# Turning gathered tokens by VectorE's 32x32 blocks in the early slots and the first main slot of a routed attention and mixture-of-experts kernel

## The chip, the cores and the metric

One core of a Trainium2 chip runs the whole kernel. The metric is the device time of one execution in microseconds (us). The engines are named as in the profile: PE is TensorE (PEld its weight loads), ACT is ScalarE, DVE is VectorE, POOL is GpSimd, and SP only issues DMAs.

## The reference

Attention with a feature map is followed by a layer of eight experts, one expert to a token. Cut to what matters:

```python
def phi(x):                        # x: 8 x 8 heads x 576 tokens x 64
    proj = x @ w_phi               # 128 features
    proj -= max(abs(proj))
    return concat(exp(proj), exp(-proj))
kv, z = phi(k).T @ v, sum(phi(k))
x = phi(q) @ kv / (phi(q) @ z + 1e-6)          # then 4608 tokens x 512

logits = x @ w_gate                            # 8 experts
# a token takes its own best expert, or, where its local gate
# is 0.5 or more, the expert of the token before it
h = relu(x @ w1[e])                            # 512 -> 1024
out = softmax(logits)[e] * (h @ w2[e])         # 1024 -> 512
```

The tokens of each expert are listed on the chip, so which tokens an expert works on is known only when the kernel runs.

## The kernel before, in words

The first part, up to about 276 us, is the attention. Its results go to a table `xs` in device memory, one row of 512 numbers to a token. After every quarter of the tokens a gate (`gate`, line 699) finds each token's expert and rank and writes its number into the lists (`lst`, line 836, from GpSimd's queue).

The second part works on slots. A slot is one expert and up to four units of 128 tokens. Two early slots of three units each use the tokens of the first half, whose gates are done, so that TensorE has work while the last gate and the plan of the main slots (`plan_main`, line 996) are computed. Then come the main slots, of four, three, two units or one.

For each unit, `gather_x` (line 1217) fetches 128 rows of `xs` by an indirect DMA of GpSimd's queue into a tile `xg`, one token to a partition. The products need the transposed form, a feature to a partition, and in two parts, a rounded high part and the rest (`xhi`, `xlo`), since each product is made of three: high by high, high by low, low by high (`three`, line 1303). There are two ways to turn a unit:

- `whole` (line 1246): TensorE turns four pieces of 128x128 into a PSUM tile `tr` (line 1252), and `parts` (line 1293) has ScalarE cast it to `xhi` (line 1299) and VectorE subtract that to give `xlo` (line 1301).
- `turned_rows` (line 1265): VectorE turns every 32x32 block of the unit in one instruction, `blocks`, into a tile `z` (line 1273). Sixteen copies of 32 partitions by 128 elements, `places`, put the blocks where they belong (line 1285), four to each of the four `j`: even `j` on GpSimd, odd `j` on ScalarE. They are done in two halves of eight. `split` then calls `parts` on the result. TensorE has no part in it.

Before the change the first early slot's three units go through `first_tokens` (line 1238) and `whole`; the second early slot's three, and the first main slot's four, go through `whole`; all later units go through `turned_rows`. That is ten units by TensorE.

A slot's weights come in eight pieces of 128x1024, four for each layer, from SP's queue (line 1157). ScalarE casts a piece to its high half `whi` (line 1170), VectorE subtracts to get `wlo` (line 1173), in `split` (line 1161). `need` (line 1207) does this for all pieces that a layer still lacks, `spare` and `landed` (lines 1186 and 1202) for those that come while a layer runs.

The order of the work around the change is written by hand. `layer1` (line 1328) goes through eight blocks f of 128 hidden features; ScalarE makes the ReLU and the high part `hh` (line 1358), VectorE the low part `hl` (line 1359). In the middle of each block, and behind its ReLU, `pause` takes the next step off a list, sixteen in all: step 2f in the middle of block f, step 2f+1 behind it. `layer2` (line 1386) takes steps at f = 0 and f = 2 of each unit, six for three units, and what is left over runs behind it. `slots` (line 1428) hands these lists over: for the early slots, `soon` for layer 1 and `later` for layer 2, built at lines 185 to 208. In `soon` of the first early slot, `go` and `rest` advance the last gate; in `soon` of the second, `read` takes the main slots' lists from TensorE and the steps `a[0]` to `a[3]` gather the first main slot's units.

Each engine works through its own queue in order. The queues are filled by a scheduler that goes by the order in which the program issues its instructions and by when it expects them to be ready. `past(engine)` (line 1181) overrides it: what stands inside is put behind the last instruction noted for that engine in `marks`. ReLUs, block copies and casts of tokens set ScalarE's mark; line 1170 issues behind it:

```python
with self.past(self.act):          # line 1169
    self.act.copy(hi, raw)
```

Of the kernel before, what the change touches and what calls it, by code (L numbers as in the profile page):

```python
# [7 lines left out]
F32 = mybir.dt.float32  # L8
# [9 lines left out]
B, H, S, D = 8, 8, 576, 64  # L18
# [63 lines left out]
class Kernel:  # L82
# [9 lines left out]
    def run(self):  # L92
        nc, tc, A = self.nc, self.tc, self.A
        act, dve = self.act, self.dve
        with ExitStack() as root:
# [94 lines left out]

            def ahead(k):
                s = self.by_size[4][0]
                self.gather_x(s, k, self.marks[self.act] if k else None)
                if k == 0:
                    self.coming.append(s)
                if k == 3:
                    m.extend(self.tokens([s], True))
            a = [lambda k=k: ahead(k) for k in range(4)]

            def more():  # L200
                next(plan, None)

            def singles():
                more()
                m[0]()
            self.slots(self.eslots, soon=[[no, no, no, go, no, no, go, no, no, go, rest],
                                          [no] * 9 + [read, a[0], a[1], no, a[2], no, a[3]]],
                       later=[[listed], [no, no, singles] + [lambda k=k: m[k]() for k in (1, 2, 3)] + [more]])
            back.close()
            self.mid.close()  # L210
            self.open_rest(root)
# [1043 lines left out]
    def tokens(self, slots, late=False, after=None):  # L1255

        for s in slots:
            if "xg" not in s:
                self.gather_x(s, after=after)
        units = [(s, k) for s in slots for k in range(s["n"])]  # L1260
        if late:
            return [lambda s=s, k=k: self.whole(s, k, k % 3 == 2, self.here()) for s, k in units]
        return [self.turned_rows(s, k) for s, k in units]

    def turned_rows(self, s, k):

        e, x = {}, s["xg"][k]
        act, dve, pool, at = self.act, self.dve, self.pool, slice(k * 128, k * 128 + 128)

        def blocks():  # L1270
            e["z"] = self.ml1.tile([128, DM], F32, name="z", bufs=2)
            with self.past(dve):
                self.marks[dve] = dve.transpose(e["z"].rearrange("p (c t) -> p c t", t=32),  # L1273
                                                x.rearrange("p (c r) -> p c r", r=32))

        def places(half):
            z = e["z"].rearrange("p (a b t) -> p a b t", a=4, b=4)
            to = self.into(s)[0].bitcast(F32)[:, :, at] if len(s["ei"]) == 2 else x.rearrange("p (a t) -> p a t", a=4)
            for j in (2 * half, 2 * half + 1):
                for b in range(4):  # L1280
                    q, g = slice(32 * b, 32 * b + 32), slice(32 * j, 32 * j + 32)
                    engine = act if j % 2 else pool
                    with self.past(engine):
                        copy = act.copy if j % 2 else pool.tensor_copy
                        self.marks[engine] = copy(to[q, :, g], z[g, :, b, :])  # L1285

        def split():
            if len(s["ei"]) == 1:
                hi, lo = [y[:, :, at] for y in self.into(s)]
                self.parts(s, hi, lo, slice(0, 128), x.rearrange("p (a t) -> p a t", a=4))  # L1290
        return blocks, lambda: places(0), lambda: places(1), split
# [136 lines left out]
    def slots(self, order, held=None, soon=(), later=()):  # L1428
# [19 lines left out]
        for i, s in enumerate(order):  # L1448
# [2 lines left out]
            self.need(s, 4)  # L1451
            new = order[i + 1] if i + 1 < len(order) else None
            rows = self.tokens(ahead[i], bool(soon) and i == 0, self.last_y if held is not None and i == 0 else None)
            first, rest = list(soon[i]) if i < len(soon) else [], rows
            if not soon and s["n"] > 1:
                some = [f for u in rows for f in u[0:3]]
                first = [lambda: None] * 16
# [146 lines left out]
```

## Time and profile before

| | us |
|---|---|
| median of 3 runs | 715.73 |
| lowest, highest run | 714.66, 718.45 |
| the profiled execution's own time | 712.14 |
| its span, first to last instruction | 710.3 |
| PE busy | 698.4 |
| DVE busy | 460.7 |
| ACT busy | 411.8 |
| POOL busy | 265.0 |

The profile is of one execution. Its span lies inside its own time; the rest is what surrounds the instructions. A row of the timeline gives the start, the duration, the engine, the line of the kernel, the operation with what it writes and reads, how often it follows itself, and in brackets how long the engine stood idle before and what ended that. TensorE's instructions overlap, so the time that one costs is read from start to start.

### The profile page before, as it was taken

The page shows a single profiled execution, that of the slowest core. Times are in us where ns is not written, and L with a number is a line of the kernel's source. Part 1 is how long each engine was busy: PE and PEld are TensorE (multiplying, and loading weights), DVE is VectorE, ACT ScalarE, POOL GpSimd, SP SyncE. Part 2 cuts the span into 40 slices and gives each one's busy share as a digit, 9 for nine tenths or more (in the row PEclk, how much of TensorE's full clock was granted, in tenths as well). Part 3 has the DMA queues.
Part 4 walks back from the last instruction along what each step waited for, and adds up shares of the span by engine and source line. Part 5 has one row for each costly group of instructions (what it writes and reads, how often), then busy time and mean ns, then how long its engine had stood idle before and what let it go on. Part 6 is the DMA issues. An engine that isn't in the chain of part 4 may idle for free. (4 is left out here: it accounts for less than half of the span.)

```text
span 710.3 us, 22974 instructions
## 1 busy us (share of the span) xinstructions
PE 698.4 (98%) x9576; PEld 617.9 (87%) x9576; DVE 460.7 (65%) x876; ACT 411.8 (58%) x888; POOL 265.0 (37%) x532
## 2 busy tenths in 40 slices
PE   7999999999999999999999999999999999999996
PEld 6999999999999999888887986889888877888985
DVE  6898899889998995683537446535643367554522
ACT  5777776777768873434465654745754269471512
POOL 0211101430146675562345551345744236443311
PEclk9999999999999999999999999999999999999998
DMA  7855545555466863254818975344886375444200
GB/s 232 268 154 148 160 124 155 148 149 161 134 183 198 252 189 113 64 181 129 280 70 294 405 279 194 135 149 150 265 307 252 110 243 172 150 163 155 76 27 31
DMA packets 66074, 125.17 MB, mean 176 GB/s; under 512 B 7180, under 2 KB 45260, under 8 KB 65910
## 3 DMA queue, kind: packets, MB, share of 16 engines
q1 hardware_dynamic: 57680, 100.90, 44.8%
q0 software_dynamic: 7968, 22.58, 9.0%
q8 instruction: 76, 1.25, 0.7%
q14 instruction: 30, 0.25, 0.1%
q10 hardware_dynamic: 320, 0.20, 0.1%
HBM read 102.11 MB, written 21.80 MB: 174 GB/s over the span
## 5 line engine op out<-in xcount | busy, mean ns | idle before, releaser
L1173 DVE TENSOR_TENSOR wlo<-wraw,whi 128x1024 fp32r<-128x1024 f32 x80 | 96.4, 1222 | 37.8 <-ACT whi L1170 37.5
L1305 PE MATMUL l<-whi,hh 128*128 128x512 f32 (+1 forms) x288 | 113.4, 394 | 0.5 <-ACT hh L1358 0.5
L1306 PE MATMUL l<-wlo,hh 128*128 128x512 f32 (+1 forms) x288 | 112.7, 391 | 0.8 <-DVE wlo L1173 0.8
L1307 PE MATMUL l<-whi,hl 128*128 128x512 f32 (+1 forms) x288 | 112.6, 391 | 0.0
L362 ACT ACTIVATE kp<-sb 128x512 f32<-128x512 f32 x144 | 83.3, 623 | 48.9 <-DVE sb L359 48.1
L1359 DVE SCALAR_TENSOR_TENSOR hl<-l,hh 128x512 fp32r<-128x512 f32 (+3 forms) x84 | 50.4, 600 | 93.2 <-ACT hh L1358 93.1
L1170 ACT CAST whi<-wraw 128x1024 fp32r<-128x1024 f32 x80 | 82.4, 1047 | 43.8 <-PE l L1307 27.0
L1358 ACT ACTIVATE hh<-l 128x512 fp32r<-128x512 f32 (+3 forms) x84 | 44.0, 525 | 108.9 <-PE l L1307 57.2
L1305 PE MATMUL l<-xhi,whi 128*128 128x384 f32 (+4 forms) x308 | 106.8, 347 | 0.0
L1307 PE MATMUL l<-xhi,wlo 128*128 128x384 f32 (+4 forms) x308 | 106.5, 346 | 0.0
L1306 PE MATMUL l<-xlo,whi 128*128 128x384 f32 (+4 forms) x308 | 106.4, 345 | 0.0
L358 DVE TENSOR_REDUCE m<-pj 128x8 f32<-128x1024 f32 (+1 forms) x74 | 88.3, 1193 | 20.4 <-PE pj L351 18.3
L1285 POOL COPY xg<-z 32x128 f32<-32x128 f32 x208 | 70.4, 339 | 58.7 <-DVE z L1273 41.4
L359 DVE TENSOR_TENSOR sb<-pj,m 128x1024 f32<-128x1024 f32 (+1 forms) x74 | 88.5, 1196 | 5.6
L351 PE MATMUL pj<-first,kq 64*128 64x128 f32 x1152 | 85.3, 289 | 3.5 <-DMA first<-in_first 3.4
L483 PE MATMUL nm<-kvs,qp 128*64 128x73 f32 x2304 | 86.3, 227 | 0.5 <-issue 0.4
L1419 POOL DMA_INDIRECT out<-y,p_tokm x31 | 37.4, 1205 | 127.2 <-DVE y L1413 126.0
L386 ACT ACTIVATE qp<-pj 128x512 f32<-128x512 f32 x144 | 78.1, 596 | 8.4 <-PE pj L371 7.5
L483 PEld LDWEIGHTS nm<-kvs,qp 128*64 128x64 f32 x2304 | 79.1, 137 | 1.0 <-issue 0.7
L351 PEld LDWEIGHTS pj<-first,kq 64*128 64x128 f32 x1152 | 71.4, 190 | 9.4 <-DMA first<-in_first 3.4
L403 PE MATMUL kvp<-v,kp 128*64 128x65 f32 x2048 | 75.3, 224 | 0.1
L1285 ACT COPY xg<-z 32x128 f32<-32x128 f32 x208 | 61.7, 296 | 20.3 <-DVE z L1273 16.0
(266 smaller groups left out, 1080.0 us busy)
## 6 DMA issues: line engine op xcount, KB each, us to landing
wraw<-in_w1h SPq DMA_DIRECT2D x44, 512.0 KB, 5.1
wraw<-in_w2h SPq DMA_DIRECT2D x44, 512.0 KB, 5.6
kq<-in_kqT SPq DMA_DIRECT2D x47, 384.0 KB, 4.1
v<-in_va SPq DMA_DIRECT2D x48, 195.0 KB, 3.5
xs<-xo SPq DMA_DIRECT2D x48, 128.0 KB, 2.4
whi<-in_w1h SPq DMA_DIRECT2D x8, 512.0 KB, 5.8
wlo<-in_w1h SPq DMA_DIRECT2D x8, 512.0 KB, 8.6
whi<-in_w2h SPq DMA_DIRECT2D x8, 512.0 KB, 7.2
```

The source lines that it names most:

```text
L351: self.last_pe = self.pe.matmul((q if j else t)[:, h, i % 2, j, :], kq[r, j, s], self.w2[r], start=True, stop=True)
L358: dve.tensor_reduce(m[:, a:a + n], x[:, s], AX.X, ALU.max, apply_absolute_value=True)
L359: self.last_dve = dve.tensor_sub(to[:, s], x[:, s], m[:, a:a + n].unsqueeze(2).broadcast_to([128, n, 128]))
L362: self.last_act = act.activation(kp[:, :, :, sg, :].rearrange("p c h f -> p h c f"), sb[:, :, :, 0], AF.Exp, scale=1.0 - 2 * sg)
L386: self.act.activation(qp[:, sg].rearrange("p h (c r k) -> p (h c) r k", c=2, r=2), src, AF.Exp, scale=1.0 - 2 * sg)
L483: self.last_num = self.pe.matmul(e["t"][r, c - c0, k], self.ch[i]["qp"][:, sg, h, q0 + r.start:q0 + r.stop], kvs[:, sg, k], start=sg == 0, ...
L1170: self.act.copy(hi, raw)
L1173: (low or self.dve).tensor_sub(lo[:, c], raw[:, c], hi.bitcast(F32)[:, c])
L1285: self.marks[engine] = copy(to[q, :, g], z[g, :, b, :])
L1305: mm(o, ah, bh, start=first, stop=False)
L1306: mm(o, ah, bl, start=False, stop=False)
L1307: self.last_pe = mm(o, al, bh, start=False, stop=last)
```

## The change

The second early slot's three units, and units 0 to 2 of the first main slot, go through `turned_rows`; unit 3 of the first main slot stays with TensorE. `turned_rows` gets a string `who` with one letter for each of the sixteen copies, in order: a for ScalarE, p for GpSimd, v for VectorE. The early units get twelve a and four v, six a and two v to each half. The main units get five p and three a in the first half, four and four in the second. The string for all later units gives the engines that they had.

The tile `z` of these units lies in the attention's memory, in place of its `kvs` tiles (`blank`). The steps are spread over the lists: the early units' blocks and halves at steps 2, 3, 5, 6, 7, 9, 10, 11 and 13 of the first early slot's layer 1, behind what stood there, and their splits in its layer 2, where `whole` stood. The gathers of the first main slot move to steps 10 to 13 of the second early slot's layer 1 and no longer wait for ScalarE's mark; unit 0's blocks and first half are step 14, its second half step 15, the last of that layer. The rest goes to the second early slot's layer 2: in the table, m is a unit's number in the first main slot.

| step of layer 2 | before | after |
|---|---|---|
| unit 0, f = 0 | nothing | m1 blocks, first half |
| unit 0, f = 2 | nothing | m1 second half |
| unit 1, f = 0 | plan goes on, m0 by TensorE | plan goes on, m2 blocks |
| unit 1, f = 2 | m1 by TensorE | m2 first half, m0 split |
| unit 2, f = 0 | m2 by TensorE | m2 second half, m1 split |
| unit 2, f = 2 | m3 by TensorE | m3 by TensorE |
| behind the layer | plan goes on | m2 split, plan goes on |

```diff
--- before.py
+++ after.py
@@ -190,22 +190,26 @@
 
             def ahead(k):
                 s = self.by_size[4][0]
-                self.gather_x(s, k, self.marks[self.act] if k else None)
+                self.gather_x(s, k)
                 if k == 0:
                     self.coming.append(s)
-                if k == 3:
-                    m.extend(self.tokens([s], True))
+                m.append(self.turned_rows(s, k, "pappappapapapapa") if k < 3 else
+                         lambda: self.whole(s, k, True, self.here()))
             a = [lambda k=k: ahead(k) for k in range(4)]
+
+            def do(*steps):
+                return lambda: [m[k][i]() for k, i in steps]
 
             def more():
                 next(plan, None)
 
             def singles():
                 more()
-                m[0]()
-            self.slots(self.eslots, soon=[[no, no, no, go, no, no, go, no, no, go, rest],
-                                          [no] * 9 + [read, a[0], a[1], no, a[2], no, a[3]]],
-                       later=[[listed], [no, no, singles] + [lambda k=k: m[k]() for k in (1, 2, 3)] + [more]])
+                m[2][0]()
+            self.slots(self.eslots, soon=[[no, no, no, go, no, no, go, no, no, go, rest] + [no] * 5,
+                                          [no] * 9 + [read, a[0], a[1], a[2], a[3], do((0, 0), (0, 1)), do((0, 2))]],
+                       later=[[listed], [do((1, 0), (1, 1)), do((1, 2)), singles, do((2, 1), (0, 3)),
+                                         do((2, 2), (1, 3)), lambda: m[3](), do((2, 3)), more]])
             back.close()
             self.mid.close()
             self.open_rest(root)
@@ -1258,17 +1262,21 @@
             if "xg" not in s:
                 self.gather_x(s, after=after)
         units = [(s, k) for s in slots for k in range(s["n"])]
-        if late:
-            return [lambda s=s, k=k: self.whole(s, k, k % 3 == 2, self.here()) for s, k in units]
-        return [self.turned_rows(s, k) for s, k in units]
-
-    def turned_rows(self, s, k):
+        return [self.turned_rows(s, k, "avaaavaaaaavaaav") if late else self.turned_rows(s, k) for s, k in units]
+
+    def blank(self):
+        if hasattr(self, "ml1"):
+            return self.ml1.tile([128, DM], F32, name="z", bufs=2)
+        z = self.back2.tile([128, 2, 2 * (KW + D + 1)], F32, name="z", tag="kvs", bufs=3)
+        return z.rearrange("p s k -> p (s k)")[:, 0:DM]
+
+    def turned_rows(self, s, k, who="ppppaaaappppaaaa"):
 
         e, x = {}, s["xg"][k]
         act, dve, pool, at = self.act, self.dve, self.pool, slice(k * 128, k * 128 + 128)
 
         def blocks():
-            e["z"] = self.ml1.tile([128, DM], F32, name="z", bufs=2)
+            e["z"] = self.blank()
             with self.past(dve):
                 self.marks[dve] = dve.transpose(e["z"].rearrange("p (c t) -> p c t", t=32),
                                                 x.rearrange("p (c r) -> p c r", r=32))
@@ -1279,9 +1287,9 @@
             for j in (2 * half, 2 * half + 1):
                 for b in range(4):
                     q, g = slice(32 * b, 32 * b + 32), slice(32 * j, 32 * j + 32)
-                    engine = act if j % 2 else pool
+                    engine, copy = {"a": (act, act.copy), "p": (pool, pool.tensor_copy),
+                                    "v": (dve, dve.tensor_copy)}[who[4 * j + b]]
                     with self.past(engine):
-                        copy = act.copy if j % 2 else pool.tensor_copy
                         self.marks[engine] = copy(to[q, :, g], z[g, :, b, :])
 
         def split():
@@ -1451,7 +1459,10 @@
             self.need(s, 4)
             new = order[i + 1] if i + 1 < len(order) else None
             rows = self.tokens(ahead[i], bool(soon) and i == 0, self.last_y if held is not None and i == 0 else None)
-            first, rest = list(soon[i]) if i < len(soon) else [], rows
+            first, rest = list(soon[i]) if i < len(soon) else [], [u[3] for u in rows]
+            if soon and rows:
+                for k, f in zip((2, 3, 5, 6, 7, 9, 10, 11, 13), [f for u in rows for f in u[0:3]]):
+                    first[k] = lambda f=f, g=first[k]: (g(), f())
             if not soon and s["n"] > 1:
                 some = [f for u in rows for f in u[0:3]]
                 first = [lambda: None] * 16
```

## Rows read from the trace of the kernel before

**Rows 1.** The page, part 1: busy us (share of the span) xinstructions
```profile
PE 698.4 (98%) x9576; PEld 617.9 (87%) x9576; DVE 460.7 (65%) x876; ACT 411.8 (58%) x888; POOL 265.0 (37%) x532
```

**Rows 2.** TensorE's waits, whole span: line, releaser, us in total, times, longest
```profile
PE l L1306 <- DVE wlo L1173: 0.8, 1, 0.8
```

**Rows 3.** Two stretches: length; busy of PE, PEld, DVE, ACT, POOL; clock, DMA, GB/s
```profile
276.00:294.00 18.00, 18.00 (x111) 17.19 (x112) 10.51 (x43) 3.60 (x8) 9.19 (x13) 1.00 0.08 23
329.20:348.00 18.80, 18.80 (x91) 15.11 (x90) 12.40 (x13) 11.69 (x16) 5.12 (x4) 1.00 0.76 232
```

**Rows 4.** Timeline: start, us, engine, line, operation, [idle before]; TensorE around one group
```profile
300.60 0.39 PE L1307 MATMUL l<-whi,hl 128*128 128x512 f32 x1
...
300.83 0.60 PE L1252 MATMUL tr<-first,xg 128*128 128x128 f32 x4
...
301.50 0.40 PE L1306 MATMUL l<-wlo,hh 128*128 128x512 f32 x1
```

**Rows 5.** Timeline, first main layer 1: ScalarE's, GpSimd's copies, VectorE's block turn
```profile
359.01 1.23 ACT L1285 COPY xg<-z 32x128 f32<-32x128 f32 x4 [7.32 <-DVE z L1273]
...
359.10 2.58 POOL L1285 COPY xg<-z 32x128 f32<-32x128 f32 x8 [5.44 <-PE l L1306]
...
358.26 0.71 DVE L1273 STREAM_TRANSPOSE z<-xg 128x512 f32<-128x512 f32 x1 [5.85 <-DMA xg<-xs,p_tokm]
```

**Rows 6.** Timeline, first early slot's layer 1: two of ScalarE's ReLUs
```profile
282.54 0.49 ACT L1358 ACTIVATE hh<-l 128x384 fp32r<-128x384 f32 x1 [1.71 <-PE l L1307]
...
287.05 0.49 ACT L1358 ACTIVATE hh<-l 128x384 fp32r<-128x384 f32 x1 [1.60 <-PE l L1307]
```

**Rows 7.** Timeline, same stretch: casts in the gate's chain on VectorE
```profile
284.64 0.22 DVE L78 CAST g_ef<-g_ci 9x128 f32<-9x128 int32 x1
...
288.05 0.19 DVE L78 CAST g_ohb<-g_oh 128x72 bf16<-128x72 f32 x1
```

**Rows 8.** Timeline, same stretch: TensorE takes the one-hot matrix
```profile
288.62 0.21 PE L780 MATMUL pt<-g_ohb,consts 128*128 128x72 bf16 x1
```

**Rows 9.** Timeline, GpSimd: the main slots' list, and unit 0's gather
```profile
316.32 0.92 POOL L902 DMA_INDIRECT lr<-lst,p_rim  x1 [0.31 <-issue]
...
323.44 0.98 POOL L1223 DMA_INDIRECT xg<-xs,p_tokm  x1 [6.20 <-DVE p_probm L673]
```

**Rows 10.** Timeline, TensorE: it takes that list
```profile
322.52 0.41 PE L933 MATMUL pt<-first,lr 34*128 34x34 f32 x2
```

**Rows 11.** Tile xg, 320 to 332 us: landing of the main slot's four gathers
```profile
DMA to landing us min/median/max: 3.3/3.3/4.2
```

**Rows 12.** Timeline, end of the second early slot's layer 1: ScalarE
```profile
329.40 0.49 ACT L1358 ACTIVATE hh<-l 128x384 fp32r<-128x384 f32 x1 [1.59 <-PE l L1307]
329.79 2.93 ACT L1170 CAST whi<-wraw 128x1024 fp32r<-128x1024 f32 x3
```

**Rows 13.** Timeline, same stretch: VectorE
```profile
327.85 0.56 DVE L1359 SCALAR_TENSOR_TENSOR hl<-l,hh 128x384 fp32r<-128x384 f32 x1 [1.52 <-ACT hh L1358]
...
330.86 3.50 DVE L1173 TENSOR_TENSOR wlo<-wraw,whi 128x1024 fp32r<-128x1024 f32 x3 [0.38 <-ACT whi L1170]
```

**Rows 14.** Timeline, same stretch: TensorE's product with the low half, its weight load
```profile
332.14 0.19 PEld L1306 LDWEIGHTS l<-wlo,hh 128*128 128x128 f32 x1 [0.21 <-DVE wlo L1173]
332.19 0.45 PE L1306 MATMUL l<-wlo,hh 128*128 128x512 f32 x1
```

**Rows 15.** Timeline at 369 us: a subtraction and a GpSimd copy
```profile
369.08 1.18 DVE L1173 TENSOR_TENSOR wlo<-wraw,whi 128x1024 fp32r<-128x1024 f32 x1
...
369.22 1.20 POOL L1285 COPY xg<-z 32x128 f32<-32x128 f32 x1 [2.51 <-DVE z L1273]
```

**Rows 16.** Timeline, end of the second early slot: last token casts; main slot's first product
```profile
344.04 1.06 ACT L1299 CAST xhi<-tr 128x512 fp32r<-128x512 f32 x2
...
348.04 1.20 PE L1349 MATMUL l<-xhi,whi 128*128 128x512 f32 x4
```

**Rows 17.** Tile xg, 349 to 358 us: landing of the next slot's gathers
```profile
DMA to landing us min/median/max: 6.5/7.2/7.8
```

## The prediction

> **What bounds the kernel now.** I read the page's busy line first: TensorE is busy 98% of a 710.3 us span and the next engine, VectorE, 65% [rows 1]. A busy TensorE could still be waiting inside its instructions, so the second view is the list of its waits. The longest after the start is 0.8 us, once, for a low half of the weights [rows 2]. So the kernel ends when TensorE has issued its queue, and a change is worth what it takes out of that queue, less the waits that it puts in. The third view is the table by stretch: in the two where the change puts its copies, the granted clock is 1.00 (the 2.4 GHz level), so no clock can be won, and ScalarE and GpSimd have room: 3.6 and 9.2 of 18.0 us busy in the first early slot's layer 1, 11.7 and 5.1 of 18.8 us in the second early slot's layer 2 [rows 3]. The question is not whether the copies fit on average but which TensorE instruction comes behind one of them.
>
> **What is removed.** A unit of 128 tokens costs TensorE four transposes. Ten units are turned this way; the change takes six: three of the second early slot, three of the first main slot. From the product ahead of a group at 300.60 to the second product behind it at 301.50 are 0.90 us, for the group and two product starts; a start is 0.23 (300.60 to 300.83) [rows 4], so the group costs 0.90 - 0.46 = 0.44. The duration printed for the group, 0.60, overlaps its neighbours and is not used. Six groups: 6 x 0.44 = **2.64 us out of TensorE's queue**. The PSUM casts and subtractions behind the groups become casts and subtractions from SBUF, as many as before, in the same place in the queues: nothing.
>
> **What is added.** Six VectorE block turns of 0.71 us and 16 block copies a unit. Four copies took ScalarE 1.23, so 0.31 each; eight took GpSimd 2.58, so 0.32 each [rows 5]. The early units get 12 ScalarE and 4 VectorE copies each, the main units 9 GpSimd and 7 ScalarE. None is on TensorE; what they cost is what they delay.
>
> **First place: the last gate's chain.** Each hidden block f of the first early slot now has a half unit behind it: six ScalarE copies, 6 x 0.31 = 1.87, and a ReLU of 0.49: 2.36 us. Two blocks took 4.51 (282.54 to 287.05), 2.26 each [rows 6]; the copies begin behind the second block, and with the unequal blocks in between the ReLU of the fifth, at 287.05, comes some 0.4 late. VectorE's subtraction for that block stands ahead of the cast of the one-hot matrix on its in-order queue. The cast ended at 288.05 + 0.19 = 288.24 [rows 7], and TensorE took it at 288.62 [rows 8]: 0.38 of cover. VectorE also gets two copies of 32x128 near there. The trace has no such copy on VectorE; below, one costs 0.15 or so like its smallest operations, above, ScalarE's 0.31; I take 0.22, from the cast of 9x128 [rows 7]. So 0.4 + 0.44 - 0.38 = **0.45 us of new TensorE wait** (0 if the copies run behind the chain, 1.3 if the lags all add). The main slots' list, which this chain feeds, was fetched from 316.32 and taken by TensorE at 322.52 [rows 9, 10]; with a landing of 4.2, the longest of the token gathers just after [rows 11], it was there at 320.5. The 2.0 of cover pay for three groups fewer ahead of it (1.32, less the new 0.45) and for a chain that is later by as much: nothing.
>
> **Second place: the split of the weights.** Line 1170 casts the high half, line 1173 subtracts the low half. For the seventh piece of the second early slot the cast began at 329.79, right behind the ReLU of the last hidden block (329.40), as first of three [rows 12]; the low half was ready after 330.86 + 3.50/3 = 332.03 [rows 13]; the product with it came at 332.19, and its weight load had waited 0.2 [rows 14]. **There is no cover at all on this chain.** The new last step of that layer 1 puts four ScalarE copies of the main slot's unit 0 behind the same ReLU and makes the last of them the mark behind which line 1170 issues. So the cast, which is ready, waits for four copies: 4 x 0.31 = 1.24. Three more stand a step earlier, behind a block turn that itself goes behind the subtraction that ended at 327.85 + 0.56 = 328.41: turned at 329.11, copied by 330.05, which holds the ReLU from 329.40 to 330.05, 0.65. Together **1.9 us of new wait**. Bounds: 1.24 if the ReLU goes ahead, 2.6 if unit 1's block turn (0.71) also slips in ahead of the subtraction. What queues behind is TensorE's whole layer 2; the next piece follows 1.17 later and is needed 1.38 later (six starts), so it adds nothing.
>
> On GpSimd and VectorE together: the last turned unit of the next stage had one GpSimd copy of 1.20 instead of 0.32, beside a weight subtraction begun at 369.08 that kept its 1.18 [rows 15]. The Trainium skill, "SBUF — State Buffer", section "Who interferes with whom", says that a VectorE instruction with two SBUF inputs and a GpSimd instruction that reads SBUF take turns, and the second to issue blocks until the first ends. By that the row agrees on GpSimd's side; on VectorE's side the subtraction could wait for one copy too, 0.3 more in the sum. I leave that to the range, since no row shows the subtraction as the loser.
>
> **Third place: the start of the main slot.** The last cast of its tokens ended at 344.04 + 1.06 = 345.1, TensorE's first product was at 348.04 [rows 16]: 2.9 us of cover. ScalarE gains 18 copies, 5.6 us on 11.7, in 18.8: it fits with 1.5 to spare. I cost this at nothing; the cover is thin, and a rival below takes it away. The gathers of these units no longer wait for ScalarE and follow each other on GpSimd, so units 1 to 3 are issued sooner: nothing.
>
> **The sum.** -2.64 + 0.45 + 1.90 = -0.29. The profiled execution took 712.14 us (span 710.3 and 1.8 around it): 711.8 by the sum. It was below the median of the runs, 715.73, by 3.59; I carry that over: **715.4**. Half a per cent, 3.6 us, is about what a measurement of this kernel can tell from no change, and even the whole 2.64 is less.
>
> **The rivals.**
> - **The full gain** (chance 0.22): neither wait comes, because the block copies of unit 0 run before the ReLU, or the queues take the cast first. For it: ScalarE was idle 1.59 us ahead of that ReLU [rows 12], time enough for five copies. Against it: the mark puts the four copies ahead. 712.14 - 2.64 = 709.5 for the profile, 713.1 as median.
> - **GpSimd is late for the main slot** (0.15), the one that ends slower. Place: the last product operand of unit 2, ahead of 348.04. GpSimd was busy 5.1 us in the 18.8; 27 copies add 8.7; if each of a slot's eight weight subtractions costs it 0.9 as in [rows 15], 7.2 more: 21.0. From 18.8 on it decides: 2.2 us of wait at the main slot's first product on top of the sum, +1.9, 717.6. Against it: some copies start before 329.2, and not every subtraction need meet one. The page of the skill named above would make this the likely outcome if all eight meet copies.
> - **Unit 0's gather lands late** (0.08). It is issued at 323.44, and those four landed in 3.3 to 4.2 us [rows 9, 11]: by 327.6, ahead of the 328.41 from which the block turn could run. From 5.0 us on the landing decides. The gathers at 350 took up to 7.8 [rows 17]; then the turn starts at 331.2, and seven copies (2.2), the ReLU, the cast and the subtraction put the low half at 336.9: a wait of 4.7 instead of 1.9, 718.2. Against: the DMA engines are little used at 323.
> - **Another order on the queues** (0.05): the change moves marks, so later instructions may be placed otherwise. Not priced; either sign.
>
> The forecast keeps 0.50.
>
> **How the numbers follow.** The forecast with its bounds (0 to 1.3, 1.24 to 2.6) spans 714.3 to 717.2. To hold 8 in 10 the range goes down to the full gain with a little scatter, 712.8, and up to the late gather, 718.2. Faster by over 0.5% would need more than the groups hold, so only scatter on the full gain: 0.06. Slower by over 0.5% needs two of the waits together or an unforeseen order: 0.09. The rest, 0.85, is within.
>
> **What would show it.** Right: 16 TensorE transposes instead of 40; a TensorE wait of 1.2 to 2.6 us for a weight's low half (or high half) in the second early slot's layer 2, with ScalarE copies between the last ReLU and the cast; under 1.3 us of waits in the gate's chain; the stretch from the second group taken to the main slot's start otherwise shorter by 0.44 a group. Wrong: no such wait (then the full gain stands), a wait of TensorE for tokens at the main slot's first product (GpSimd), or a gain over 2.64 us, which nothing here explains.

## The result, and the profile after

The change made the kernel slower: 723.37 us as median of 7 runs (721.33 to 725.44) beside 717.61 of 7 runs of the kernel before (714.45 to 718.86), a ratio of 1.0098 with a 95% interval of 1.0073 to 1.0122. Here and below the ratio comes with its interval from the single runs; it is not the quotient of the two medians. The profiled execution took 723.37 us, its span 721.6. Forecast was no change that a measurement can tell.

The page of the kernel after, part 1 (busy us, share of the span, xinstructions), answers to [rows 1]:

```profile
PE 700.7 (97%) x9552; PEld 619.3 (86%) x9552; DVE 467.6 (65%) x894; ACT 428.8 (59%) x945; POOL 280.1 (39%) x559
```

TensorE issues 24 instructions fewer, so all six groups are gone, and still its busy time is up by 2.3: part of it ran at a lower clock, below. Lines have moved by 4 up to about line 1262 and by 8 behind it. TensorE's waits in the kernel after (line, releaser, us in total, times, longest), beside [rows 2]:

```profile
PE pt L937 <- DMA lr<-lst,p_r: 6.5, 1, 6.5
PE pj L355 <- DMA first<-in_first: 3.4, 1, 3.4
PE l L1313 <- ACT y L1423: 2.0, 1, 2.0
PE pt L937 <- DMA lr<-lst,p_rim: 0.8, 1, 0.8
PE l L1313 <- ACT whi L1174: 0.7, 1, 0.7
PE l L1315 <- issue: 0.7, 1, 0.7
PE pt L771 <- DVE g_ef L78: 0.4, 1, 0.4
```

The second one is the start of the kernel and was there before. The one that was forecast is the fifth, 0.7 for a weight's high half. The longest, 6.5, is for a list that the prediction never mentions: `p_r`, the rows of the last slots, fetched by `more` inside `singles` in the second early slot's layer 2 and handed to TensorE by the last step of that layer (`more` again). GpSimd's timeline, first of the kernel before, at the end of the second early slot:

```profile
336.01 1.02 POOL L1419 DMA_INDIRECT out<-y,p_toke  x1 [4.90 <-ACT y L1415]
337.33 1.88 POOL L902 DMA_INDIRECT lr<-lst,p_r  x1 [0.30 <-issue]
```

The same in the kernel after:

```profile
334.41 0.94 POOL L1293 COPY xg<-z 32x128 f32<-32x128 f32 x3 [0.90 <-DVE z L1281]
336.40 14.72 POOL L1293 COPY xg<-z 32x128 f32<-32x128 f32 x24 [1.05 <-DMA xg<-xs,p_tokm]
351.40 1.03 POOL L1427 DMA_INDIRECT out<-y,p_toke  x1 [0.28 <-POOL xg L1293]
352.73 1.03 POOL L906 DMA_INDIRECT lr<-lst,p_r  x1 [0.30 <-issue]
```

Before, the fetch stood 10.4 us ahead of TensorE's use of the list at 347.72. After, 24 block copies stand ahead of it on GpSimd's in-order queue, it is issued at 352.73, and TensorE, which had finished its layer, waits for it. Of the 15.4 us by which the fetch is later, 4.4 are the later start of the whole slot (first product at 316.43 for 312.00); 11.0 are its own. The copies are slow as well: 14.72 for 24, where 24 x 0.32 [rows 5] would be 7.7. The tile `xg` from 336 to 352 us (ns, min/median/max) shows how:

```profile
L1293 POOL COPY xg<-z x24: 285/289/1357, 336.4 to 349.8; 32x128 f32<-32x128 f32 x24
L1293 ACT COPY xg<-z x18: 294/296/300, 335.8 to 351.2; 32x128 f32<-32x128 f32 x18
```

Sixteen GpSimd copies keep 0.29; eight take 0.66 to 1.36. Those are the ones that meet one of VectorE's subtractions, six of the weights and two of the tokens, one copy to each. GpSimd's and VectorE's timeline, same stretch:

```profile
338.05 2.75 POOL L1293 COPY xg<-z 32x128 f32<-32x128 f32 x3
...
338.15 2.49 DVE L1177 TENSOR_TENSOR wlo<-wraw,whi 128x1024 fp32r<-128x1024 f32 x2 [0.54 <-ACT whi L1174]
```

Two subtractions of 1.25 each, and three copies in the same 2.75. The subtraction all but keeps its time (1.18 in [rows 15]). The Trainium skill, "SBUF — State Buffer", "Who interferes with whom", has a GpSimd instruction that reads SBUF and a VectorE instruction with two SBUF inputs exclude each other, and ScalarE never wait on anyone; both agree with these rows, ScalarE's 18 copies staying within 294 to 300 ns.

Behind the wait the products run slowly. TensorE, kernel after, with the next list and the three first blocks of the main slot:

```profile
359.26 0.38 PE L937 MATMUL pt<-first,lr 22*128 22x22 f32 x2 [6.51 <-DMA lr<-lst,p_r]
359.57 2.08 PE L1357 MATMUL l<-xhi,whi 128*128 128x512 f32 x4
361.44 1.91 PE L1357 MATMUL l<-xhi,wlo 128*128 128x512 f32 x4
363.15 1.46 PE L1357 MATMUL l<-xlo,whi 128*128 128x512 f32 x4
364.45 0.39 PE L1313 MATMUL l<-xhi,whi 128*128 128x512 f32 x1
```

And the table by stretch there (length; busy of PE, PEld, DVE, ACT, POOL with instructions; clock, DMA share, GB/s):

```profile
358.50:364.50 6.00, 5.24 (x15) 4.19 (x16) 0.27 (x2) 0.00 (x0) 3.14 (x4) 0.55 0.81 294
```

The granted clock is 0.55 on the mean, mostly the lower level of 1.2 GHz. Twelve products took 364.45 - 359.57 = 4.88, where they took 350.89 - 348.04 = 2.85 before: 2.0 us more.

By stages, from first product to first product: the first early slot took 36.13 before and 40.07 after (+3.9), the second 36.04 and 43.14 (+7.1), the main slot's twelve products 2.0 more. The second slot's +7.1 is 6.5 + 0.8 + 0.7 of waits less three groups; 0.5 is not accounted for. The three stages together are 13.0, more than the 11.3 between the spans; the remainder of the span was about 2 us shorter, and why is open. The first slot's +3.9 has waits of 0.4, 0.7 and 2.0 in it, the last of them here:

```profile
309.24 0.74 PE L1313 MATMUL l<-whi,hh 128*128 128x512 f32 x1 [1.98 <-ACT y L1423]
```

Behind it the granted clock was 0.50 from 309.3 to 312.7 us, which is some 1.7 more. How much of this is the change's is told by the runs.

### The profile page after: what moved, and what is told of

It is laid out like the page before. It is cut to its first block, busy times and chain, and to the rows that moved or that the text cites. A ratio compares the mean times of both kernels' runs of the same rounds, so it can differ in the third digit from the quotient of the medians.

```text
span 721.6 us, 23029 instructions
## 1 busy us (share of the span) xinstructions
PE 700.7 (97%) x9552; PEld 619.3 (86%) x9552; DVE 467.6 (65%) x894; ACT 428.8 (59%) x945; POOL 280.1 (39%) x559
## 3 DMA queue, kind: packets, MB, share of 16 engines
q8 instruction: 76, 1.25, 0.7%
## 5 line engine op out<-in xcount | busy, mean ns | idle before, releaser
L366 ACT ACTIVATE kp<-sb 128x512 f32<-128x512 f32 x144 | 83.3, 623 | 50.8 <-DVE sb L363 43.1
L1293 POOL COPY xg<-z 32x128 f32<-32x128 f32 x235 | 86.8, 369 | 62.0 <-DVE z L1281 43.8
L1293 ACT COPY xg<-z 32x128 f32<-32x128 f32 x265 | 78.5, 296 | 15.5 <-DVE z L1281 10.1
L390 ACT ACTIVATE qp<-pj 128x512 f32<-128x512 f32 x144 | 78.1, 595 | 8.6 <-PE pj L375 7.9
```

The costliest lines, as they stand in the source:

```text
L366: self.last_act = act.activation(kp[:, :, :, sg, :].rearrange("p c h f -> p h c f"), sb[:, :, :, 0], AF.Exp, scale=1.0 - 2 * sg)
L390: self.act.activation(qp[:, sg].rearrange("p h (c r k) -> p (h c) r k", c=2, r=2), src, AF.Exp, scale=1.0 - 2 * sg)
```

## The experiments

Four sets of kernels were run, each set together on one chip with the kernel before. The kernel before had a median of 715.45 (13 runs), 713.34 (24), 712.52 (28) and 716.98 (23) there.

**First set: the whole change again, and its two halves.** The first has no edit.

> The changed kernel once more, unaltered. In its first profile two things are to be told apart: TensorE's wait of 6.5 us for the last list (lr), and a stretch from 302.7 to 308.5 us in which VectorE's short operations of the plan come 0.5 us apart with one gap of 2.3, ScalarE's first output takes place at 308.50, and TensorE waits 0.7 and 2.0 us. Theory A: both belong to the order of the queues and come again, each within 0.5 us. Theory B: the stretch at 302.7 is a chance of that execution; then here VectorE's plan runs without gaps over 0.5 us there, TensorE has no wait of over 0.5 us between 296 and 312, and the time is some 3 to 4 us less.

724.65 us; the wait for the list 5.9, half the clock again behind it, for the other list 1.1, and the stretch is there again. Theory A, with the list's wait 0.6 apart where 0.5 was allowed.

For the next, the main slot goes back to TensorE:

```diff
-                m.append(self.turned_rows(s, k, "pappappapapapapa") if k < 3 else
-                         lambda: self.whole(s, k, True, self.here()))
+                m.append(lambda: self.whole(s, k, k % 3 == 2, self.here()))
-                m[2][0]()
+                m[0]()
```

with the gathers and steps of before.

> Only the second early slot's units go by blocks; the first main slot's by TensorE, as before. Theory (GpSimd's queue): the loss comes from the main units' copies on GpSimd, so the wait for the last list is gone here; three groups out of TensorE's queue are 1.3 us, the gate's chain puts 0.4 back: 0.5 to 1 us under the kernel before if the waits at 302 to 309 don't come. Rival (the early copies): these cost as much as in the changed kernel's first profile, 0.4 + 0.7 + 2.0 of waits and 1.7 of lower clock, less 1.3: 3 to 4 us over the kernel before.

718.45, ratio 1.0038 (1.0015 to 1.0062); no wait for `p_r`, but 1.1 for the list `p_rim` and waits of 0.3 to 1.0 in several other places. It is 3.0 over the kernel before, the rival's time. For the third, the early units go back to TensorE:

```diff
-        return [self.turned_rows(s, k, "avaaavaaaaavaaav") if late else self.turned_rows(s, k) for s, k in units]
+        if late:
+            return [lambda s=s, k=k: self.whole(s, k, k % 3 == 2, self.here()) for s, k in units]
+        return [self.turned_rows(s, k) for s, k in units]
```

and the lines that spread their steps over layer 1 are taken out.

> Only units 0 to 2 of the first main slot go by blocks; the second early slot's units by TensorE, as before. Theory (GpSimd's queue): the fetch of the last list stands behind 24 copies in a row again, TensorE waits 5 to 7 us for it, loses some 2 us more at the lower clock, and has 1.3 less to do: 5 to 8 us over the kernel before. Rival (the early copies make everything late): TensorE's wait for that list is under 1 us and the time within 2 us of the kernel before.

721.79, ratio 1.0084 (1.0060 to 1.0108), with a wait of 5.0 for `p_r` and half the clock behind it, 6.3 over the kernel before, as the theory had it. The main units by themselves make most of the loss. In the fourth the list's step goes ahead of the copies:

```diff
+            def fourth():
+                a[3]()
+                more()
             def singles():
-                more()
-                                          [no] * 9 + [read, a[0], a[1], a[2], a[3], do((0, 0), (0, 1)), do((0, 2))]],
+                                          [no] * 9 + [read, a[0], a[1], a[2], fourth, do((0, 0), (0, 1)), do((0, 2))]],
```

> The changed kernel, with the fetch of the last list issued with the gather of unit 3, ahead of all main copies on GpSimd, instead of behind them. Nothing else is taken away. Theory (GpSimd's queue): TensorE's 6.5 us wait for that list goes, and the lower clock behind it with it: 7 to 9 us less than the changed kernel, which leaves 0 to 3 over the kernel before. Rival (unit 2's copies on GpSimd end too late whatever the list does, or ScalarE's queue does): TensorE then waits 4 us or more for xhi at the main slot's first product instead, and the time stays within 3 us of the changed kernel's.

720.85, ratio 1.0084 (1.0063 to 1.0106). TensorE takes the list without a wait and then waits for unit 2's operand:

```profile
352.45 0.39 PE L940 MATMUL pt<-first,lr 22*128 22x22 f32 x2
355.66 2.07 PE L1360 MATMUL l<-xhi,whi 128*128 128x512 f32 x4 [2.81 <-DVE xlo L1312]
```

The list's wait is gone as foreseen, but not the 7 to 9 us: the time is 3.8 under the one run of the whole change above and 5.4 over the kernel before. The rival's 4 us of wait for unit 2 are 2.8. So the list was the last of two late things. The 24 copies are late for the main slot too, by 2.8, and the half clock (2.07 for four products) comes behind that wait as well.

**Second set: the copies moved off GpSimd.** The kernel before, unedited:

> The kernel before once more, unaltered, for its trace. The changed kernel and all three parts of it showed a stretch of 5.7 us, some 26 us into the first early slot, in which VectorE's short operations come 0.5 us apart, ScalarE's first output takes place late, and TensorE waits 0.8 to 3 us; the one profile of the kernel before had none, and was 3.5 us under the median of its runs. Theory A: the stretch belongs to every ordinary execution, the one profile was lucky: then it is here too, and the profile of this run takes 714 to 717 us. Theory B: the change's copies bring it about: then it is absent here and the profile takes 712 to 713.

711.77 us; stages of 36.15 and 36.02. The first set's profiles had all shown a stretch between 302 and 308 us, in the first early slot, where VectorE's small operations of the plan come 0.3 to 2.3 us apart; it is not in this one, nor in any other profile of this set. Then the third kernel with GpSimd's copies by VectorE:

```diff
-                m.append(self.turned_rows(s, k, "pappappapapapapa") if k < 3 else
+                m.append(self.turned_rows(s, k, "vavvavvavavavava") if k < 3 else
```

> Only units 0 to 2 of the first main slot go by blocks, as in the run that had that part alone, but the 27 copies of GpSimd are made by VectorE. Theory (GpSimd's queue): the list's fetch stands behind no copy, TensorE's wait of 5 us for it goes and the lower clock with it; what stays is 0.7 for the weight cast behind ScalarE's copies, against 1.3 less work: 6 to 7 us under the run with GpSimd's copies, within 1 us of the kernel before. Rival (the copies as such are too much for the stretch, whoever makes them): VectorE's 6 us more make weights or tokens late, TensorE waits 3 us or more for wlo or xlo, and the time stays 4 us or more over the kernel before.

715.92, ratio 1.0025 (1.0010 to 1.0041). No wait for `p_r`, nor the half clock; 0.7 for a weight's high half; and at the main slot's first product:

```profile
351.22 1.19 PE L1359 MATMUL l<-xhi,whi 128*128 128x512 f32 x4 [2.53 <-DVE xlo L1311]
```

It is 2.6 over the kernel before, between what the theory and the rival allowed: the list and the clock were GpSimd's, and the copies as such are late too.

That kernel with unit 0's copies moved out of layer 1, behind the casts of the weights:

```diff
-                                          [no] * 9 + [read, a[0], a[1], a[2], a[3], do((0, 0), (0, 1)), do((0, 2))]],
-                       later=[[listed], [do((1, 0), (1, 1)), do((1, 2)), singles, do((2, 1), (0, 3)),
+                                          [no] * 9 + [read, a[0], a[1], a[2], a[3], no, no]],
+                       later=[[listed], [do((0, 0), (0, 1)), do((0, 2), (1, 0)), singles, do((2, 0), (2, 1), (0, 3)),
```

with `m[2][0]()` replaced by `do((1, 1), (1, 2))()`.

> As the run before it, and unit 0's block turn and copies are issued in layer 2, behind the casts of the last weight pieces, not at the end of layer 1. Theory (the mark on ScalarE): the wait of 0.7 us of TensorE for a weight's high half at the seventh piece goes too; 0.7 us less than the run before it, 0.5 to 1.5 under the kernel before. Rival: unit 2 is then late for the main slot's first product: a wait for xhi or xlo of 1 us or more there.

715.61, ratio 1.0025 (1.0010 to 1.0039). The wait for the high half is gone, as foreseen, and the end is later by as much:

```profile
352.74 2.07 PE L1359 MATMUL l<-xhi,whi 128*128 128x512 f32 x4 [3.46 <-ACT xhi L1309]
```

This is the rival. Three units of copies between the casts and subtractions do not get done in time in this slot, neither with GpSimd and ScalarE nor with VectorE and ScalarE. Last of the set, the early units with nothing in place of TensorE:

```diff
-            if soon and rows:
-                for k, f in zip((2, 3, 5, 6, 7, 9, 10, 11, 13), [f for u in rows for f in u[0:3]]):
-                    first[k] = lambda f=f, g=first[k]: (g(), f())
```

> The second early slot's units are neither turned by TensorE nor by blocks: their block turns and copies are left out and the gathered rows are split as they are, so the products of that slot are on tokens that are not turned. The main slot is as before. Theory (the copies delay the gate's chain): without them TensorE has no wait for g_ef or g_ohb, and the time is 1 to 1.5 us under the kernel before; the early part's loss of 3 us is then its copies. Rival (TensorE only comes earlier to what is late anyway): the waits behind the first unit's output and for the main slots' list stay, 2 us or more together, and the time is within 1 us of the kernel before.

712.30, ratio 0.9997 (0.9980 to 1.0015). The first early slot takes 34.70, 1.45 less for three groups, and TensorE waits for the main slots' list instead:

```profile
322.98 0.38 PE L935 MATMUL pt<-first,lr 34*128 34x34 f32 x2 [1.99 <-DMA lr<-lst,p_rim]
```

This is the rival: no wait in the gate's chain, and nothing won.

**Third set: what recurs elsewhere.** The whole change, unedited:

> The whole change once more, beside runs of the kernel before. Theory A (its loss is the wait for the last list behind GpSimd's copies, about 6 us with the half clock behind it, and comes wherever the kernel runs): a TensorE wait of 5 to 7 us for the list read from p_r, ratio 1.007 to 1.012. Theory B (the stretch of slow operations near 305 us in the first job's profiles made it, and this goes with the job): if that stretch is missing here, the wait for the list falls under 4 us and the ratio under 1.005.

717.73, ratio 1.0072 (1.0057 to 1.0087): slower without the stretch too. Its first early slot takes 34.67, with no wait in the gate's chain at all. TensorE's waits:

```profile
PE pt L937 <- DMA lr<-lst,p_r: 6.1, 1, 6.1
...
PE l L1313 <- ACT whi L1174: 0.7, 1, 0.7
...
PE pt L937 <- DMA lr<-lst,p_rim: 0.7, 1, 0.7
```

The early units alone, as in the first set:

> The early units' part alone once more. Theory A (six copies behind each hidden block delay the gate's chain, and what TensorE gains it gives back at the main slots' list): TensorE waits of 0.3 to 0.6 us for the gate's casts, one of 0.5 to 2 us for the list read from p_rim, ratio 0.999 to 1.003. Theory B (its 1.0038 belonged to the first job's slow stretch): ratio 0.998 to 1.000, no wait for the gate's casts over 0.2 us.

710.66, ratio 0.9974 (0.9958 to 0.9990): faster by 1.9 us, more than either theory allowed. The two first products of the early slots, 34.70 apart:

```profile
277.57 0.98 PE L1355 MATMUL l<-xhi,whi 128*128 128x384 f32 x4
...
312.27 0.87 PE L1355 MATMUL l<-xhi,whi 128*128 128x384 f32 x4
```

No wait for the gate's casts, 0.4 for the list. Then two main units instead of three, with all copies of the main units in layer 2, as in the second set:

```diff
-                m.append(self.turned_rows(s, k, "vavvavvavavavava") if k < 3 else
-                         lambda: self.whole(s, k, True, self.here()))
+                m.append(self.turned_rows(s, k, "vavvavvavavavava") if k < 2 else
+                         lambda: self.whole(s, k, k == 2, self.here()))
```

> Only units 0 and 1 of the first main slot by blocks, copies by VectorE and ScalarE, in the second early slot's layer 2; units 2 and 3 by TensorE, the early units too. Theory A (three units are too many for the stretch, two fit): no TensorE wait over 0.8 us at the main slot's first product, two groups of 0.44 us won, time 0.3 to 1.1 us under the kernel before, ratio 0.9985 to 0.9996. Theory B (any copies between the casts delay the main slot's operands): a wait of 1 us or more at its first product, ratio 1.000 to 1.002.

712.91, ratio 1.0018 (1.0006 to 1.0029): theory B. ScalarE and TensorE at the start of the main slot:

```profile
344.59 1.05 ACT L1174 CAST whi<-wraw 128x1024 fp32r<-128x1024 f32 x1 [1.61 <-DMA wraw<-in_w2h]
345.55 1.06 ACT L1309 CAST xhi<-tr 128x512 fp32r<-128x512 f32 x2
346.50 1.06 ACT L1174 CAST whi<-wraw 128x1024 fp32r<-128x1024 f32 x1
...
347.64 1.16 PE L1359 MATMUL l<-xhi,whi 128*128 128x512 f32 x4 [1.10 <-ACT whi L1174]
```

Now a cast of the weights comes last, two token casts and a landing of weights ahead of it. Last, the main units with nothing in place of TensorE:

```diff
-                if k == 3:
-                    m.extend(self.tokens([s], True))
+                m.append(self.turned_rows(s, k)[3] if k < 3 else lambda: self.whole(s, k, False, self.here()))
```

> The kernel before with TensorE's turning of units 0 to 2 of the first main slot taken out and nothing in its place: the casts take the gathered rows as they are, so the rows of these units enter the products unturned and the output is not the reference's. No block turns, no copies, the gathers where they were. Theory A (a group is worth 0.44 us and nothing else holds up TensorE there): 1.3 us under the kernel before, ratio 0.9978 to 0.9986, no new wait. Theory B (as with the early slot, something else is then waited for): ratio 0.999 to 1.001, with a new TensorE wait of 0.5 us or more between 325 and 350 us.

710.75, ratio 0.9976 (0.9966 to 0.9985): theory A. No new wait comes between 325 and 350 us; one of 0.8 for `hl` comes in the main slot, at 361. The second early slot takes 34.57:

```profile
312.10 0.87 PE L1348 MATMUL l<-xhi,whi 128*128 128x384 f32 x4
...
346.67 1.20 PE L1348 MATMUL l<-xhi,whi 128*128 128x512 f32 x4
```

The gain of the main groups is there, 1.45 in the slot (36.04 and 36.02 in two profiles of the kernel before); the copies lose it.

**Fourth set: the sign of the early part.** The early units alone, a third time:

> The early units' part alone, a third time. Theory A (the part by itself saves TensorE three groups, and only the stretch of slow VectorE operations near 305 us, where a run has it, turns that into a loss): without that stretch in the profile the first early slot takes 34.6 to 34.8 us, the list read from p_rim is waited for 0.3 to 0.8 us, ratio 0.996 to 0.999; with it the slot takes over 39 us, ratio 1.002 to 1.006. Theory B (the difference between the two jobs is chance): slot and ratio don't go together so.

718.05, ratio 1.0020 (0.9998 to 1.0042); the stretch is there, and the first early slot takes 40.05. The kernel before beside it:

> The kernel before, one look in the same job. Theory A: it has the slow stretch where the early units' part has it, and then its first early slot takes 37 to 38 us; where that has none, 36.1. Theory B: the two profiles differ in this.

715.14 us, with the stretch, its first early slot 37.24. And the early part without its copies:

> The early units' turning by TensorE taken out with no block turns and no copies in its place, a second time; the second early slot's products take the gathered rows unturned, so the output is not the reference's. Theory A (the copies as such cost nothing; what is won stands against the wait for the list read from p_rim): ratio within 0.002 of that of the kernel with the copies in this job, a wait for that list of 0.5 to 2 us. Theory B (the copies' delays of the gate's chain matter): this one is 1 us or more below the one with copies.

717.51, ratio 1.0002 (0.9981 to 1.0023), with the stretch, and in place of a wait for the list 3.3 us for the second slot's `xlo`. It is 0.5 below the kernel with the copies, inside either interval. Its two early slots take 35.90 and 42.20, 78.1 together, with the copies 76.9: the loss beside the stretch is not the copies'. The table by stretch from 302 to 308 us (columns as above), the kernel before in the second set:

```profile
302.00:308.00 6.00, 6.00 (x30) 4.91 (x30) 5.96 (x28) 2.52 (x4) 5.09 (x4) 1.00 0.26 64
```

The kernel before in the fourth set:

```profile
302.00:308.00 6.00, 5.45 (x25) 3.95 (x25) 2.48 (x26) 0.90 (x2) 2.89 (x3) 1.00 0.05 12
```

The early units alone, fourth set:

```profile
302.00:308.00 6.00, 4.78 (x21) 3.49 (x19) 1.77 (x14) 0.00 (x0) 3.57 (x4) 1.00 0.37 122
```

VectorE is busy 5.96 of 6.00 us in the first and 2.48 and 1.77 in the others; the profile puts its idle time mostly down to VectorE's own operations or to "issue", which is nothing that it shows. So the stretch goes with the set, not with the change: the kernel before has it too. The two profiles of the result are an exception that matters: the kernel before lacks the stretch there (VectorE 5.97 busy) and the kernel after has it (1.58), so part of the first slot's +3.9 is the stretch's and not the change's. It costs the kernel before 1.1 us of its first early slot (37.24 for 36.13), and the kernel with the early units by blocks 5.4 (40.05 for 34.70). The sign of the early part goes with it: -1.9 us in the one set without the stretch, +3.0 and +1.1 in the two with it, the +1.1 not clear of noise. That the stretch turns the sign is read from these three sets; no run switches it on or off. What makes it is open; the second set, without it, and the first ran on the same chip.

## Why the prediction was wrong

**Removed: right, and a little larger.** Forecast was 0.44 a group. Three groups shortened the first early slot by 1.45 in one kernel without copies and in two with them (34.70, 34.67 and 34.70 for 36.15), and the second by 1.45 without copies: 0.48 each, 2.9 for six.

**First place, 0.45: there in some sets only.** In the two profiles of the third set with the early copies there is no wait in the gate's chain: the bound of 0. In the five profiles with these copies that have the stretch, the profile after among them, TensorE waited 0.3 to 0.5 for `g_ef`, a step ahead of the one-hot matrix, and in two of them 0.5 more for `g_ohb`: 0.3 to 1.1, inside the bounds. This wait comes near 288 us, ahead of the stretch at 302, and profiles with the stretch and without these copies do not have it. Why it came in these and not in the third set is open.

**The main slots' list, "nothing": wrong, by the fetch and not by the cover.** I took its landing as 4.2 from the gathers. It was shorter: in the kernel without copies TensorE took the list 3.75 behind its fetch, 322.98 less 319.23. By that the cover before was 322.52 - 320.07 = 2.4, enough for a TensorE that came 1.2 to 1.4 earlier. But I held the fetch fixed. Counted from the first product of the first early slot, it was issued at 40.4 before and at 42.1 to 43.5 in the three profiles without the stretch in which the early groups are gone. GpSimd in the kernel without copies:

```profile
314.14 0.92 POOL L904 DMA_INDIRECT lr<-lst,p_rih  x1 [3.94 <-DVE p_jm L78]
...
319.23 0.92 POOL L904 DMA_INDIRECT lr<-lst,p_rim  x1 [0.30 <-issue]
```

An earlier fetch on GpSimd's queue, that of `p_rih`, at 309.30 before, stands behind VectorE's `p_jm` now, and this one behind it: 1.99 of wait; with the copies 0.4 and 0.7. It is not the copies' doing: the three kernels of the second and third set that have main copies and early units by TensorE fetch the list at 43.1 to 43.4 too, and the kernel before without the main groups at 40.5. Which line of the edit moved it was not isolated.

**Second place, 1.9: right mechanism, mis-sized (0.72).** The cast did stand behind the unit's last four copies, as the timeline of ScalarE in the kernel after shows:

```profile
334.38 0.91 ACT L1293 COPY xg<-z 32x128 f32<-32x128 f32 x3 [1.25 <-DVE z L1281]
335.31 0.49 ACT L1366 ACTIVATE hh<-l 128x384 fp32r<-128x384 f32 x1
335.83 1.22 ACT L1293 COPY xg<-z 32x128 f32<-32x128 f32 x4
337.07 2.00 ACT L1174 CAST whi<-wraw 128x1024 fp32r<-128x1024 f32 x2
```

Before, the ReLU came 0.20 behind the first product of layer 2 (329.40 and 329.20); after, that product was at 334.52 and the ReLU at 335.31, 0.59 late (forecast 0.65). The cast is 1.96 late by the same reckoning (forecast 1.9). TensorE's timeline around the seventh piece:

```profile
337.05 0.39 PE L1315 MATMUL l<-whi,hl 128*128 128x512 f32 x1
338.17 0.74 PE L1313 MATMUL l<-whi,hh 128*128 128x512 f32 x2 [0.72 <-ACT whi L1174]
338.75 0.40 PE L1314 MATMUL l<-wlo,hh 128*128 128x512 f32 x1
338.98 0.40 PE L1315 MATMUL l<-whi,hl 128*128 128x512 f32 x1
339.22 0.40 PE L1313 MATMUL l<-whi,hh 128*128 128x512 f32 x1
339.47 0.50 PE L1314 MATMUL l<-wlo,hh 128*128 128x512 f32 x1
```

The product with the low half is the last row. In the kernel's order of before it follows the product with the high half at once; after, the scheduler has put four products of the next unit in between, from pieces that were there. They cost no time of their own, so of the 1.9 only the wait for the high half was left, 0.72 in the list of waits. Moving the copies away took that away too. What was wrong in this term is that I held TensorE's order fixed and took "Another order on the queues" as a rival without a price.

**Third place, "nothing": the step that failed.** I asked whether ScalarE's copies fit, and left GpSimd's 27 to a rival. That rival's working was good: 7.2 of extra time for copies that meet subtractions, measured 14.72 - 7.7 = 7.0 for 24. But it looked for who waits at one place, the main slot's operands. It never listed what stood behind the copies on GpSimd's queue. The fetch of `p_r` was put behind 24 copies and went from 337.33 to 352.73, 25.3 and 36.3 behind the slot's first product; TensorE came for the list at 352.75, and 6.5 from issue to use became 6.5 of wait where 10.4 of lead had been. The runs show it from both sides: the wait went when the fetch was put ahead of the copies, and when VectorE made them. The place named by the rival is real, 2.8 us with the list out of the way (2.5 and 3.5 with VectorE's copies), but it hides behind the list.

**The clock, "no clock can be won": none won, but 2.0 lost.** I had not priced what a long wait does to the products behind it.

Taken from the rows without the stretch (the whole change in the third set): -2.9 + 0.7 (main slots' list) + 0.7 (cast) + 6.1 (last list) + 2.4 (half clock, (358.18 - 352.89) - 2.85) = 7.0. Its two early slots and the main slot's twelve products are 7.6 longer than before, so 0.6 is not accounted for. Between the medians are 5.2 (717.73 less 712.52), between that profile's span and the one of before 6.4; the 1.2 to 2.4 left over lie in the rest of the span and stay open. The forecast was -0.29: it lacked the last list and the half clock behind it, 8.5 together, and had the cast at 1.9 for 0.7. A slip beside that: its bounds add up to 717.0 at the upper end, not 717.2.

The version that beat both is the early part alone, 710.66 beside 712.52 and 717.73 in the third set; it did so in that set alone, and in the two with the stretch it was slower than before or not to be told from it.

## What to carry to other kernels

Work moved off a busy engine onto an idle one is priced by the idle engine's queue, not by its idle time: write down each instruction that the new work is put ahead of, small DMAs first, and who waits for it. When an engine gets faster, look up in the new profile when each thing that it receives from elsewhere is issued; cover read from the old profile holds only while the issuing queue keeps its order. And take a term's sign from several sets of runs, when the gain is 2 us and a stretch of the program varies by more.

## What the hardware showed that was not expected

- Behind a wait of TensorE of 2.81, 3.46, 5.0 or 6 us at the end of the second early slot the next products came at the 1.2 GHz level (four in 2.07 instead of 1.2); behind one of 2.53 they did not (1.19). A wait of 6.5 us so cost 8.5. The length of one wait does not tell it alone: in the first early slot of the kernel after, waits of 0.7 and 2.0 close together were followed by a clock of 0.50.
- A GpSimd block copy takes 0.29 by itself and up to 1.36 beside a weight subtraction of 1.23, while the same copies on ScalarE stay at 0.30.
- Between 302 and 308 us VectorE's chain of small operations had gaps of 0.2 to 2.3 us in all kernels of two sets, in one of them the kernel before too, and none in those of two others. The time of the kernel before was 715.45 and 716.98 in the sets with it, 713.34 and 712.52 in those without.
